# Moving the low parts of all split weights to VectorE, with a new port rule and other planned durations, in a windowed attention and MLP kernel

## The chip, the cores and the metric

The kernel runs on one core of a Trainium2 chip. The time is the device time of one execution in microseconds (us), the median of several runs. Engine names in the profile: PE is TensorE, PEld its weight loads, DVE is VectorE, ACT is ScalarE, POOL is GpSimd, SP is SyncE, which issues all DMAs. "L459" is line 459 of the kernel's file.

## The reference, cut to what matters

Inputs: q, k, v of (4, 8, 768, 64) in fp32, eight memory keys and values per head, and two weight matrices, w_in of (512, 2048) and w_out of (2048, 512).

```
for each chunk c of 32 queries:
    keys, values = 8 memory rows + rows (c*32 - 16) to (c*32 + 40), cut at the ends
    a = exp(scores - max);  a = a / (sum(a) + 1e-9)        scores = q k^T / 8
    attention[c] = a @ values
x = attention as (3072 tokens, 512)
h = x @ w_in;  g = s * relu(h)^2 + b;  out = g @ w_out      all fp32
```

## The kernel before, in words

**Data.** Attention is done in blocks of 96 queries against 128 keys (three chunks and a mask), two heads and four blocks at a time: that is one `attend(ch, c)`. Tokens are in eight chunks of 384 (`ch`), each of which needs four `attend` calls (`c`). The MLP runs over 16 blocks `f` of 128 hidden units; a step `(ch, f)` has a first product (`hidden`, L472, 12 matmuls) and a second (`result`, L494, 9 matmuls).

**Split in two parts.** The MLP's products are made of fp32r operands, each fp32 value being kept as a high part, rounded by a copy on ACT, and a low part, the value less its high part. There are three matmuls for each product: low by high, high by low, high by high. So there are low parts of x (L394, DVE), of g (L483, DVE) and of the weights (L459, DVE or POOL).

**Weights.** They come as 64-bit words (the host's arrays are viewed as int64 and passed as they are). `weight(i, half, f, due)` makes one tile of 128 x 512 from them: a DMA (L447), a scaled copy of the high word on ACT (L449, `wscale`), three integer operations on DVE (L450 `wlow`, L452 `wjoin`, L454 `wsign`), the high part on ACT (L458, `whigh`) and the low part (L459). There are 32 such tiles: half 0 is w_in, half 1 is w_out. In the kernel before, the low part is taken by DVE for the eight tiles of half 0 with f under 8, and by POOL (under the name `wrest`) for the other 24. The source words live in a ring of four buffers, the joined fp32 values in a ring of three (`wv`), which a tile holds from L449 to L459. Sixteen of the finished tiles lie in slots that earlier held source data.

**Attention.** One `attend` has score matmuls (L371), mask, maximum and shift in one custom DVE operation (L402), an exponential on ACT (L406), then for the normalisation a small POOL operation (L409), a reciprocal on DVE (L411) and a product on POOL (L412, `norm`). The probabilities are turned by PE and copied (L421, L424, L426) for the first two chunks, and by DVE block transposes (L432) for the others. Then come the value matmuls (L388) and the two parts of x (L393, L394). g is made by four ACT operations (L479 to L482) and one on DVE (L483).

**Order.** The instructions of each engine are in the order in which a planner written in the kernel (`Plan.lay`) lays them out, while the kernel is built. Each operation has an engine, a duration (`HOLD`), a priority (small is urgent) and dependences; a result is usable on another engine `LATE` ns after its operation's end. At each moment the planner goes through PE, ACT, DVE, POOL, SP, and gives an engine that is free its most urgent ready operation whose buffers can be had. Operations marked `lock` (L409, L412, the weights' operations on DVE, and L459) are those that need the SBUF port that DVE and POOL share; the planner never lays a locked operation of one of the two while a locked one of the other runs. On the chip nothing enforces that order between the two engines but data dependences: each engine runs its own list in order.

**Priorities.** A step's products and its g have its number u in the list of steps as priority (`result` 1.9 later). Steps are: chunk 0 with f 0 to 7 (u 0 to 7), chunk 1 with f 0 to 15 (u 8 to 23), chunk 0 with f 8 to 15, then the chunks 2 to 7. A weight tile has f + half - 1.5, so every weight is more urgent than the g of a step from u = 15 on, and those of f are more urgent than the g of step 8 + f. The normalisations of chunk 1 have -1.25 to 5.25, those of chunk 2 from 16.75 on. Until 40 us of the plan, empty moments of PE are filled with matmuls of no use (L296).

Of the kernel before, what the change touches and what calls it, by code (L numbers as in the profile page):

```python
# [52 lines left out]
         + [(ch, f) for ch in range(2, NCHUNK) for f in range(NF)])  # L53


HOLD = dict(hidden=527, result=705, scores=225, turn=110, value=165, warm=215, sums=470, total=950,
            relu=388, square=388, affine=570, high=388, xhigh=388, wscale=571, whigh=536, copy=270, exp=386, keep=388, store=480, bias=500,
            low=475, affine_v=475, rec=100, max=212, flip=316, xlow=470, wlow=336, wjoin=600, wsign=605, out=600,
            small=120, norm=1000, wrest=1250, issue=440)
LATE = dict(PE=200, ACT=150, DVE=130, POOL=100, SP=0)  # L60
RATE, LAND = 400.0, 2000.0
FLIGHT = 8
BEGIN = dict(PE=2500.0, ACT=2500.0, DVE=2500.0, POOL=2500.0, SP=800.0)
# [47 lines left out]
class Plan:  # L111
# [5 lines left out]
    def op(self, eng, kind, prio, fn, reads=(), writes=(), lock=False, size=0):  # L117
        o = Op()
        o.eng, o.hold, o.fn, o.prio, o.lock, o.n, o.size = eng, HOLD[kind], fn, prio, lock, len(self.ops), size
        o.deps, o.outs, o.vals = set(), [], []  # L120
# [16 lines left out]
    def lay(self, filler=None):  # L137

        for o in self.ops:
            o.left, o.ready, o.start = len(o.deps), 0.0, None  # L140
            for d in o.deps:
                d.outs.append(o)
        engines = ["PE", "ACT", "DVE", "POOL", "SP"]
        free = dict(BEGIN)
        lock = {"DVE": 0.0, "POOL": 0.0}
        waiting = {e: [] for e in engines}
        ready = {e: [] for e in engines}
        events = sorted(BEGIN.values())
        wire, flying = 0.0, []
        laid = []  # L150
        back = []
        for o in self.ops:
            if not o.left:
                heapq.heappush(waiting[o.eng], (0.0, o.n, o))
        todo = len(self.ops)
        while todo:
            t = heapq.heappop(events)
            while events and events[0] <= t:
                heapq.heappop(events)
            while back and back[0][0] <= t:  # L160
                v = heapq.heappop(back)[-1]
                v.ring.back(v)
            for e in engines:
                while waiting[e] and waiting[e][0][0] <= t:
                    o = heapq.heappop(waiting[e])[2]
                    heapq.heappush(ready[e], (o.prio, o.n, o))
                if free[e] > t:
                    continue
                if e == "SP":
                    flying = [x for x in flying if x > t]  # L170
                    if len(flying) >= FLIGHT:
                        heapq.heappush(events, min(flying))
                        continue
                put, got = [], None
                while ready[e]:
                    x = heapq.heappop(ready[e])
                    o = x[2]
                    new = [v for v in o.vals if v.slot is None and v.ring.tiles is not None]
                    held = o.lock and e in lock and lock["POOL" if e == "DVE" else "DVE"] > t
                    given = []  # L180
                    for v in new if not held else ():
                        if not v.ring.can(v):
                            break
                        v.ring.give(v)
                        given.append(v)
                    if not held and len(given) == len(new):
                        got = o
                        break
                    for v in reversed(given):
                        v.ring.undo(v)  # L190
                    if held:
                        heapq.heappush(events, lock["POOL" if e == "DVE" else "DVE"])
                    put.append(x)
                for x in put:
                    heapq.heappush(ready[e], x)
                if got is None:
                    if e == "PE" and filler and filler[0](t):
                        laid.append((t, -1, filler[1]))
                        free[e] = t + HOLD["warm"]
                        heapq.heappush(events, free[e])  # L200
                    continue
                o = got
                o.start = t
                free[e] = t + o.hold
                o.end = free[e] + LATE[e]
                if o.size:
                    wire = max(wire, t) + o.size / RATE
                    o.end = wire + LAND
                    flying.append(o.end)
                if o.lock and e in lock:  # L210
                    lock[e] = free[e]
                laid.append((t, o.n, o.fn))
                todo -= 1
                heapq.heappush(events, free[e])
                for d in o.outs:
                    d.left -= 1
                    d.ready = max(d.ready, free[e] if d.eng == e and not o.size else o.end)
                    if not d.left:
                        heapq.heappush(waiting[d.eng], (d.ready, d.n, d))
                        heapq.heappush(events, d.ready)  # L220
                for v in o.vals:
                    v.left -= 1
                    v.done = max(getattr(v, "done", 0.0), o.end)
                    if not v.left and v.ring.tiles is not None:
                        heapq.heappush(back, (v.done, o.n, o.vals.index(v), v))
                        heapq.heappush(events, v.done)
            if not events and todo:
                stuck = [(o.eng, o.prio, [v.kind for v in o.vals if v.slot is None]) for e in engines for _, _, o in ready[e]]
                raise AssertionError(f"the plan is stuck at {t}: {todo} left, {stuck[:12]}")
        self.end = max(o.end for o in self.ops)  # L230
        laid.sort(key=lambda x: (x[0], x[1]))
        return laid
# [3 lines left out]
def body(ctx: ExitStack, tc: tile.TileContext, qkv, w1, w2, s_in, b_in, out):  # L236
    nc = tc.nc
    plan = Plan()
    op = plan.op
# [14 lines left out]
    def weight_tile(half, f):  # L254
        if (half, f) not in wts:
            i = LATE_W.index((half, f)) if (half, f) in LATE_W else -1
            wts[half, f] = const.tile([P, 2, DM], F32R, name=f"w{half}_{f}", tag=f"slot{i}" if i >= 0 else f"w{half}_{f}")
        return wts[half, f]
# [180 lines left out]
    def weight(i, half, f, due):  # L439
        src = (w1, w2)[half][f]  # L440
        raw = Early(i, 0, 2 * DM) if i < NEARLY - 6 else Val(words)
        v, w = Val(wvs), c_w[half, f]
        both = lambda: raw.tile.bitcast(I32).rearrange("p (n two) -> p n two", two=2)
        lo, hi = (lambda: both()[:, :, 0]), (lambda: both()[:, :, 1])
        bits = lambda: v.tile.bitcast(I32)
        dst = lambda a: weight_tile(half, f)[:, a, :]
        op("SP", "issue", due - 4, lambda: nc.sync.dma_start(both(), src), (), (raw["lo"], raw["hi"]), size=P * DM * 8)  # L447

        op("ACT", "wscale", due, lambda: nc.scalar.activation(v.tile, hi().bitcast(F32), AF.Copy, scale=2.0 ** -112), (raw["hi"],), (v[0],))  # L449
        op("DVE", "wlow", due, lambda: nc.vector.tensor_scalar(lo(), lo(), 29, None, ALU.logical_shift_right),  # L450
           (), (raw["lo"],), lock=True)
        op("DVE", "wjoin", due, lambda: nc.vector.scalar_tensor_tensor(bits(), bits(), 3, lo(), ALU.logical_shift_left, ALU.bitwise_or),  # L452
           (raw["lo"],), (v[0],), lock=True)
        op("DVE", "wsign", due, lambda: nc.vector.scalar_tensor_tensor(bits(), hi(), -2147483648, bits(), ALU.bitwise_and, ALU.bitwise_or),  # L454
           (raw["hi"],), (v[0],), lock=True)
        rest = half or f >= N0
        old = list(c_early[LATE_W.index((half, f))].parts.values()) if (half, f) in LATE_W else []
        op("ACT", "whigh", due, lambda: nc.scalar.activation(dst(0), v.tile, AF.Copy), (v[0],), [w["H"], *old])  # L458
        op(("DVE", "POOL")[rest], ("wjoin", "wrest")[rest], due, lambda: (nc.vector, nc.gpsimd)[rest].tensor_tensor(  # L459
            dst(1), v.tile, dst(0).bitcast(F32), ALU.subtract), (v[0], w["H"]), (w["L"],), lock=True)  # L460


# [57 lines left out]
    for i, (due, half, f) in enumerate(ORDER):  # L520
        weight(i, half, f, due - 1.5)
# [49 lines left out]
```

## Time and profile before

| | |
|---|---|
| median of 3 runs | 658.1 us (657.54 to 658.69) |
| the profiled execution | 656.1 us, span 654.3 us |
| mean granted clock of TensorE | 0.992 of full speed |
| busy in the span: PE, DVE, ACT, POOL | 97%, 55%, 64%, 19% |

The profiled execution is one run; its span goes from the first to the last instruction, and 1.8 us of its time lie around the span. Busy shares over the span hide that the stages have different limits.

### The profile page before, as it was taken

To read this page: it belongs to the slowest core of one execution; us is meant where nothing else is said; L and a number is where in the kernel's file an instruction comes from. 1 tells how busy PE (TensorE), PEld (TensorE's weight loads), DVE (VectorE), ACT (ScalarE), POOL (GpSimd) and SP (SyncE) were. 2 spreads that over 40 slices of the span, in tenths; PEclk is the share of its full clock that TensorE was granted. 3 is DMA by queue.
4 is the path that set the end of the run, shared out by engine and by line. 5 is a ranking of instruction groups with operands and counts; after the bars stand their busy time and mean duration, and the time that the engine had idled before them with its cause. 6 is when DMAs were issued, how large, how long until landed. Compare 5 with 4: busy or idle time off the path is not lost.

```text
span 654.3 us, 10859 instructions
## 1 busy us (share of the span) xinstructions
PE 636.6 (97%) x3833; PEld 548.4 (84%) x3833; DVE 357.4 (55%) x1258; ACT 421.4 (64%) x1137; POOL 121.5 (19%) x168
## 2 busy tenths in 40 slices
PE   9999877999999999999999999999999999999996
PEld 5677766888888888888888888888888888889995
DVE  5899979872255545565455545555454655441112
ACT  6999898755466655566665656666655666655442
POOL 5544544340011011111101011110101111100000
PEclk9999989899999999999999999999999999999999
DMA  8933654200202110120112111021110210010001
GB/s 295 404 146 111 207 174 157 82 1 0 82 30 93 44 46 20 42 89 33 46 46 81 38 35 46 29 94 45 45 43 19 94 29 16 2 49 1 1 1 49
DMA packets 17623, 46.84 MB, mean 72 GB/s; under 512 B 2208, under 2 KB 2208, under 8 KB 17568
## 3 DMA queue, kind: packets, MB, share of 16 engines
q1 hardware_dynamic: 17568, 46.15, 20.6%
q8 instruction: 30, 0.49, 0.3%
q14 instruction: 25, 0.20, 0.1%
HBM read 39.85 MB, written 6.29 MB: 71 GB/s over the span
## 4 chain that ended last, share of the span: by engine, by line
PE 84%; DVE 7%; ACT 5%; DMA 2%; issue 1%; POOL 0%; SPq 0%; DVEq 0%; ACTq 0%
PE ps L494 37%; PE ps L472 37%; PE ps L371 5%; PE ps L388 4%; DVE wv L454 2%; DVE wv L452 2%; PE ps L296 1%; ACT t L406 1%; DVE words L450 1%; DMA early<-qkv 1%; ACT w L458 1%; PE ps L421 1%; ACT ps L481 1%; DMA words<-w 1%; ACT wv L449 1%
## 5 line engine op out<-in xcount | busy, mean ns | idle before, releaser
L472 PE MATMUL ps<-xH,w 128*128 128x384 f32 x1024 | 262.7, 338 | 1.5 <-DVE w L459 1.5
L494 PE MATMUL ps<-w,gH 128*128 128x512 f32 x768 | 242.1, 397 | 0.0
L472 PEld LDWEIGHTS ps<-xH,w 128*128 128x128 f32 x1024 | 187.1, 189 | 7.5 <-DVE w L459 2.0
L472 PE MATMUL ps<-xL,w 128*128 128x384 f32 x512 | 177.2, 346 | 0.0
L494 PEld LDWEIGHTS ps<-w,gH 128*128 128x128 f32 x768 | 145.6, 190 | 28.1
L494 PE MATMUL ps<-w,gL 128*128 128x512 f32 x384 | 156.2, 407 | 7.6 <-DVE gL L483 7.6
L479 ACT ACTIVATE ps<-ps 128x384 f32<-128x384 f32 x128 | 60.8, 475 | 150.8 <-PE ps L472 150.7
L483 DVE TENSOR_TENSOR gL<-ps,gH 128x384 fp32r<-128x384 f32 x128 | 71.3, 557 | 132.8 <-ACT gH L482 130.6
L432 DVE STREAM_TRANSPOSE aT<-t 32x128 f32<-32x128 f32 x384 | 116.2, 302 | 50.2 <-POOL t L412 45.5
L406 ACT ACTIVATE t<-t,nmax 96x128 f32<-96x128 f32 x256 | 99.1, 391 | 9.4 <-DVE nmax L402 9.4
L472 PEld LDWEIGHTS ps<-xL,w 128*128 128x128 f32 x512 | 96.8, 189 | 9.0 <-ACT w L458 0.3
L494 PEld LDWEIGHTS ps<-w,gL 128*128 128x128 f32 x384 | 72.6, 189 | 24.5 <-DVE gL L483 9.6
L402 DVE CUSTOM_DVE_ANT_0 t<-ps,mask 96x128 f32<-96x128 f32 x256 | 58.9, 280 | 56.6 <-PE ps L371 55.6
L481 ACT ACTIVATE ps<-ps,b_sb,s_sb 128x384 f32<-128x384 f32 x128 | 82.5, 644 | 4.1
L412 POOL TENSOR_TENSOR t<-t,rden 96x512 f32<-96x512 f32 x64 | 69.4, 1086 | 65.5 <-DVE rden L411 65.5
L409 POOL TENSOR_SCALAR rden<-den 96x4 f32<-96x4 f32 x64 | 15.7, 245 | 331.8 <-ACT t L406 329.1
L482 ACT ACTIVATE gH<-ps 128x384 fp32r<-128x384 f32 x128 | 62.8, 491 | 3.6
L480 ACT ACTIVATE ps<-ps 128x384 f32<-128x384 f32 x128 | 60.9, 476 | 3.8
L406 ACT ACTIVATION_READ_ACCUMULATOR t<-t,nmax 96x1 f32 x256 | 48.7, 190 | 0.0
L459 POOL TENSOR_TENSOR w<-wv,w 128x512 fp32r<-128x512 f32 x24 | 33.1, 1385 | 53.3 <-ACT w L458 53.3
L393 ACT ACTIVATE xH<-ps 128x384 fp32r<-128x384 f32 x32 | 15.7, 490 | 41.3 <-PE ps L388 40.8
L371 PE MATMUL ps<-raw 64*96 64x128 f32 x448 | 32.5, 280 | 0.0
(47 smaller groups left out, 321.8 us busy)
## 6 DMA issues: line engine op xcount, KB each, us to landing
raw<-qkv SPq DMA_DIRECT2D x28, 448.0 KB, 3.4
words<-w SPq DMA_DIRECT2D x22, 512.0 KB, 3.5
v<-qkv SPq DMA_DIRECT2D x28, 256.0 KB, 2.7
out<-partial SPq DMA_DIRECT2D x21, 256.0 KB, 2.6
early<-w SPq DMA_DIRECT2D x10, 512.0 KB, 9.4
early<-qkv SPq DMA_DIRECT2D x4, 448.0 KB, 6.5
early<-qkv SPq DMA_DIRECT2D x4, 256.0 KB, 6.8
out<-wv SPq DMA_DIRECT2D x3, 256.0 KB, 2.0
```

What stands on the lines that cost most here:

```text
L371: nc.tensor.matmul(scv(n)[:, j, :], raw.tile[rows, j * QB:(j + 1) * QB], raw.tile[rows, TOK + j * P:TOK + (j + 1) * P], start=True, stop=True)
L402: op("DVE", "max", a + 0.1, lambda j=j: nc.vector.tensor_tensor_reduce(t.tile[:, j, :], scv()[:, j, :], mask[:, half, j], -SCALE, 3.0e38, ...
L406: op("ACT", "exp", a + 0.2, lambda j=j: nc.scalar.activation(t.tile[:, j, :], t.tile[:, j, :], AF.Exp, bias=nmax()[:, j:j + 1], scale=-1.0 ...
L412: op("POOL", "norm", a + 0.25, lambda: nc.gpsimd.tensor_tensor(t.tile, t.tile, rden().unsqueeze(2).to_broadcast([QB, GB, P]), ALU.mult), [ ...
L432: nc.vector.transpose(aT.tile[gg, :, cs], t.tile[cs, :, gg])
L472: nc.tensor.matmul(h.tile[:, :TOK], weight_tile(0, f)[:, wi, c * P:(c + 1) * P], x.tile[xi], start=(c == 0 and n == 0), stop=(c == NC_T - ...
L479: op("ACT", "relu", u, lambda: nc.scalar.activation(hp(), hp(), AF.Relu), (), (h[0],))
L480: op("ACT", "square", u, lambda: nc.scalar.activation(hp(), hp(), AF.Square), (), (h[0],))
L481: op("ACT", "affine", u, lambda: nc.scalar.activation(hp(), hp(), AF.Identity, scale=s_sb, bias=b_sb), (c_s[0], c_b[0]), (h[0],))
L482: op("ACT", "high", u, lambda: nc.scalar.activation(g.tile[0], hp(), AF.Copy), (h[0],), (g["H"],))
L483: op("DVE", "low", u, lambda: nc.vector.tensor_tensor(g.tile[1], hp(), g.tile[0].bitcast(F32), ALU.subtract), (h[0], g["H"]), (g["L"],))
L494: nc.tensor.matmul(acc.tile, g.tile[gi][:, t * P:(t + 1) * P], weight_tile(1, f)[:, wi, :], start=(first and n == 0), stop=(last and n == 2))
```

## The change

All 32 low parts of weights (L459) are on DVE, under the planner's name `wjoin`. The planner gets a rule: a locked operation of DVE or POOL is put back if the other of the two engines is free and has a ready locked operation with a smaller priority. `HOLD` and `LATE` are changed in some 15 places: `turn`, `value`, `small`, `rec`, `hidden` and others a few to 120 ns, and `LATE` up by 30 to 50 ns. `rest` is left without use.

```
-            low=475, affine_v=475, rec=100, max=212, flip=316, xlow=470, wlow=336, wjoin=600, wsign=605, out=600,
-            small=120, norm=1000, wrest=1250, issue=440)
-LATE = dict(PE=200, ACT=150, DVE=130, POOL=100, SP=0)
+            low=475, affine_v=475, rec=120, max=212, flip=316, xlow=470, wlow=345, wjoin=610, wsign=612, out=600,
+            small=240, norm=1010, wrest=1290, issue=440)
+LATE = dict(PE=230, ACT=180, DVE=180, POOL=150, SP=0)
...
-                    held = o.lock and e in lock and lock["POOL" if e == "DVE" else "DVE"] > t
+                    other = "POOL" if e == "DVE" else "DVE"
+                    held = o.lock and e in lock and lock[other] > t
+
+                    if o.lock and e in lock and free[other] <= t and any(y[2].lock and y[:2] < x[:2] for y in ready[other]):
+                        put.append(x)
+                        continue
...
-        op(("DVE", "POOL")[rest], ("wjoin", "wrest")[rest], due, lambda: (nc.vector, nc.gpsimd)[rest].tensor_tensor(
+        op("DVE", "wjoin", due, lambda: nc.vector.tensor_tensor(
             dst(1), v.tile, dst(0).bitcast(F32), ALU.subtract), (v[0], w["H"]), (w["L"],), lock=True)
```

In the first line of `HOLD`, `hidden` goes from 527 to 535, `result` from 705 to 712, `scores` from 225 to 222, `turn` from 110 to 84 and `value` from 165 to 185.

## Rows read from the trace of the kernel before

**Rows 1.** Windows by stage: PE, PEld, DVE, ACT, POOL busy, clock, DMA share, GB/s.

```profile
40.00:76.00 36.00, 34.20 (x228) 28.02 (x228) 34.40 (x103) 34.48 (x97) 17.68 (x17) 1.00 0.38 127
76.00:136.00 60.00, 50.12 (x264) 43.08 (x263) 50.84 (x108) 47.12 (x121) 26.98 (x23) 0.91 0.39 131
136.00:649.00 513.00, 512.24 (x3021) 451.23 (x3020) 240.26 (x898) 307.42 (x804) 57.51 (x91) 1.00 0.12 39
```

**Rows 2.** Waits of PE from 76 to 136 us: total, times, longest.

```profile
PE ps L494 <- DVE gL L483: 6.8, 4, 2.7
PE ps L388 <- DVE gL L483: 1.7, 1, 1.7
```

**Rows 3.** Timeline of PE, the matmuls that follow its longest gaps.

```profile
81.32 0.38 PE L388 MATMUL ps<-aT,v 128*64 128x96 f32 x2 [1.66 <-DVE gL L483]
...
90.68 0.50 PE L494 MATMUL ps<-w,gL 128*128 128x512 f32 x1 [2.14 <-DVE gL L483]
...
112.88 0.80 PE L494 MATMUL ps<-w,gL 128*128 128x512 f32 x1 [2.74 <-DVE gL L483]
...
135.53 0.50 PE L494 MATMUL ps<-w,gL 128*128 128x512 f32 x1 [1.29 <-DVE gL L483]
```

**Rows 4.** Windows with the clock below full, columns as in rows 1.

```profile
100.00:120.00 20.00, 16.60 (x69) 14.31 (x69) 18.84 (x52) 15.08 (x43) 7.92 (x7) 0.83 0.34 119
...
114.00:116.00 2.00, 2.00 (x6) 1.55 (x5) 1.93 (x12) 2.00 (x5) 0.51 (x2) 0.50 0.32 115
```

**Rows 5.** Groups of instructions by line: busy us, mean ns, idle before and its releaser.

```profile
L459 POOL TENSOR_TENSOR w<-wv,w 128x512 fp32r<-128x512 f32 x24 | 33.1, 1385 | 53.3 <-ACT w L458 53.3
L459 DVE TENSOR_TENSOR w<-wv,w 128x512 fp32r<-128x512 f32 x8 | 5.5, 684 | 0.0
```

**Rows 6.** The weights' DVE operations by line: shortest, median and longest ns.

```profile
L450 DVE TENSOR_SCALAR words<-words x22: 415/423/1530, 46.0 to 132.1; 128x512 int32<-128x512 int32 x22
L452 DVE SCALAR_TENSOR_TENSOR wv<-wv,words x22: 676/686/1595, 56.8 to 132.6; 128x512 int32<-128x512 int32 x22
L454 DVE SCALAR_TENSOR_TENSOR wv<-words,wv x22: 681/693/1800, 57.5 to 133.4; 128x512 int32<-128x512 int32 x22
```

**Rows 7.** Timeline of DVE: a moved operation's pace, and operations beside POOL.

```profile
46.05 1.86 DVE L450 TENSOR_SCALAR words<-words 128x512 int32<-128x512 int32 x2
...
71.15 0.68 DVE L459 TENSOR_TENSOR w<-wv,w 128x512 fp32r<-128x512 f32 x1
71.75 0.28 DVE L402 CUSTOM_DVE_ANT_0 t<-ps,mask 96x128 f32<-96x128 f32 x1
...
73.86 1.41 DVE L454 SCALAR_TENSOR_TENSOR wv<-words,wv 128x512 int32<-128x512 int32 x1
...
76.52 1.52 DVE L450 TENSOR_SCALAR words<-words 128x512 int32<-128x512 int32 x1
78.14 1.59 DVE L452 SCALAR_TENSOR_TENSOR wv<-wv,words 128x512 int32<-128x512 int32 x1
...
133.35 1.66 DVE L454 SCALAR_TENSOR_TENSOR wv<-words,wv 128x512 int32<-128x512 int32 x1
134.93 0.55 DVE L483 TENSOR_TENSOR gL<-ps,gH 128x384 fp32r<-128x384 f32 x1
```

**Rows 8.** Timeline of POOL beside the operations of rows 7.

```profile
73.24 1.49 POOL L412 TENSOR_TENSOR t<-t,rden 96x512 f32<-96x512 f32 x1
76.02 3.17 POOL L459 TENSOR_TENSOR w<-wv,w 128x512 fp32r<-128x512 f32 x2 [1.29 <-ACT w L458]
```

**Rows 9.** Waits of DVE and of ACT from 76 to 136 us.

```profile
DVE gL L483 <- ACT gH L482: 4.9, 4, 2.1
...
ACT w L458 <- DVE wv L454: 8.5, 7, 2.2
```

**Rows 10.** Windows of L459, then of L412, alone: busy time and count, DVE then POOL.

```profile
76.00:136.00 60.00, 0.00 (x0) 22.86 (x17) 0.91 0.39 131
...
40.00:136.00 96.00, 11.41 (x9) 0.95 0.38 130
```

More of the change, by code (lines that the diff above doesn't have):

```diff
@@ L53 @@
          + [(ch, f) for ch in range(2, NCHUNK) for f in range(NF)])
-HOLD = dict(hidden=527, result=705, scores=225, turn=110, value=165, warm=215, sums=470, total=950,
+HOLD = dict(hidden=535, result=712, scores=222, turn=84, value=185, warm=215, sums=470, total=950,
             relu=388, square=388, affine=570, high=388, xhigh=388, wscale=571, whigh=536, copy=270, exp=386, keep=388, store=480, bias=500,
-            low=475, affine_v=475, rec=100, max=212, flip=316, xlow=470, wlow=336, wjoin=600, wsign=605, out=600,
-            small=120, norm=1000, wrest=1250, issue=440)
-LATE = dict(PE=200, ACT=150, DVE=130, POOL=100, SP=0)
+            low=475, affine_v=475, rec=120, max=212, flip=316, xlow=470, wlow=345, wjoin=610, wsign=612, out=600,
+            small=240, norm=1010, wrest=1290, issue=440)
+LATE = dict(PE=230, ACT=180, DVE=180, POOL=150, SP=0)
 RATE, LAND = 400.0, 2000.0
@@ L191, in lay @@
                     if held:
-                        heapq.heappush(events, lock["POOL" if e == "DVE" else "DVE"])
+                        heapq.heappush(events, lock[other])
                     put.append(x)
```

## The prediction

> **What bounds the kernel now.** I read the stages first, since 97% busy over the whole span says nothing about one stage. From 136 to 649 us PE is busy for 512.24 of 513 us at full clock [rows 1]: nothing that DVE or POOL gain there can move the end, and only the last weight operation reaches into it. What can be won or lost lies before. From 40 to 76 us PE, DVE and ACT are all full (34.20, 34.40 and 34.48 of 36 us). From 76 to 136 us PE has only 50.12 of 60 us, at a mean clock of 0.91, while DVE still has 50.84 and ACT 47.12 [rows 1]. So this stage loses 9.9 us of PE to waits and 60 x 0.09 = 5.4 us to the clock, about 15 us together; that is the whole prize, apart from the first 40 us.
>
> Next I read who is waited for. From 76 to 136 us 8.5 us are for the low part of g (L483 on DVE), five times [rows 2]. The timeline puts them in a few gaps: 1.66, 2.14, 2.74 and 1.29 us [rows 3], and one of 0.7 us that is left of the sum, at 101 us. The clock falls behind the two longest: 0.83 from 100 to 120 us [rows 4], which is 20 x 0.17 = 3.4 us, and the other 2 us behind the gap that ends at 90.68 us. Before the fall PE had stood idle, and the first matmul after the 2.74 us gap takes 0.80 us where its like after other gaps take 0.50 [rows 3]. PE at half clock, 0.50 from 114 to 116 us [rows 4], 1.2 in place of 2.4 GHz, is the second price of a gap.
>
> Then why L483 is late. Two low parts of weights on POOL (76.02 us, 3.17 us for both [rows 8]) run beside two operations of DVE that take 1.52 and 1.59 us [rows 7], where their medians are 0.42 and 0.69 [rows 6]: DVE stood still for 1.1 + 0.9 = 2.0 us, with L483 queued behind. So with a like pair at 108 us, before the longest gap, and in a smaller way at 133.35 us, where a 0.69 us operation takes 1.66 us and L483 starts right behind it [rows 6, 7]. From 76 to 136 us there are nine such rows, with 8.7 us over the medians in all; one more is at 46 us, where two L450 take 1.86 us [rows 7], some 1.1 us over two that run alone. The second chain is ACT's: it waits 8.5 us for L454 [rows 9], which these stretches delay, and L483 then waits 4.9 us for ACT's high part.
>
> **The change, part by part.**
>
> *Low parts to DVE.* POOL loses 24 operations of 1385 ns, 33.1 us [rows 5]. DVE gets 24 of 684 ns; the next operation starts 0.60 us after such a one (71.15 to 71.75 [rows 7]), so they cost its queue 24 x 0.60 = 14.4 us. It gets back the 9.8 us of stretches. Net: 4.6 us more on DVE. This has to be split by stage.
>
> Seven of the 24 lie before 76 us and 17 behind [rows 10]. The seven: 7 x 0.60 = 4.2 us more, 1.1 us back, so 3.1 us more in a stage where DVE has 36 - 34.40 = 1.6 us free [rows 1]. What doesn't fit is 1.5 us at least, 3.1 us if no free moment can be used; PE is nearly full here as well, with work that is due soon, so I charge it: +2 us, between 1.5 and 3.1.
>
> The 17: 17 x 0.60 = 10.2 us more, 8.7 us back, 1.5 us more, against 9.2 us in which DVE has nothing to run [rows 1]. The load fits. What counts is when. A stretch of 2.0 us for two low parts becomes 1.2 us of DVE work that the planner knows of and can lay behind L483, or ahead of it. The gaps whose cause is a stretch are 1.66, 0.7, 2.74 and 1.29 us, 6.4 us, with 3.4 us of clock after the longest: 9.8 us. If the new operations all stand in front of L483, 40% of it (0.8 of 2.0) comes back, 3.9 us; if none does, all of it. Weights are more urgent to the planner than most of these g, which speaks for the lower end; but a shorter gap may also spare the clock, which is a step and not a slope. I take two thirds: -6.5 us, between -3.9 and -9.8.
>
> *A new wait.* A low part on DVE waits for ACT's high part (L458) at the head of DVE's queue, where POOL could stand idle for 53.3 us at no cost; behind it stand L402 and L483, and PE waits for these. The eight that are on DVE now found their input ready: 0.0 idle [rows 5]. I take nothing for it, as those eight; the upper bound is a wait like L458's own, 8.5 / 7 = 1.2 us [rows 9], for a few of them.
>
> *Normalisations.* They stay on POOL. They stretch DVE too: 1.41 for 0.69 us at 73.86 us, beside L412 taking 1.49 us [rows 7, 8]. With a fuller DVE a few more meet; there are nine between 40 and 136 us [rows 10], so from 0 to 9 x 0.7 = 6 us of DVE, of which the trace shows about 3 already. I take 0 more, and the rest goes to the range. The port is thus one thing that either engine holds at a time: the 1.52 us operation begins 0.5 us after POOL's pair and ends after POOL's first. The Trainium skill (SBUF — State Buffer, Who interferes with whom) has it that the second to issue blocks fully until the first is done, also for a DVE operation with two SBUF inputs; the stretch of 1.1 us agrees. By that rule the moved operations can themselves be blocked, at the price just bounded.
>
> *The port rule and the other durations.* Before, the planner looks at DVE first, so a run of weight operations could keep an urgent normalisation back in the plan, though not on the chip. Now it is laid earlier, and PE's turn and value matmuls with it. The changes of 10 to 120 ns reorder single operations. No row prices a reordering. The bound from both sides is the worst single gap with its clock, 2.74 + 3.4 = 6.1 us; I take 0, since PE's long stage has 0.8 us idle in 513 and each g has two steps of slack.
>
> *Queues.* SP's weight DMAs wait for L454 to free a word buffer; with fewer stretches they start earlier, into a DMA share of 0.39 [rows 1]. The joined values' buffers are held for 0.7 in place of 1.4 us at the end. Both are cover, not gain. No DMA is added.
>
> Sum: +2 - 6.5 = -4.5 us. The profiled execution has 656.1 us (span 654.3), so 651.6 us on its scale; it is 2.0 us below the median of the runs, 658.1 us, and the change is put on that: **653.6 us**.
>
> **Rivals.**
>
> *Slower: DVE becomes the bound.* The weights end at 136 us because DVE's queue ends then. Its load rises by 4.6 us, and from 40 to 76 us there is no room. If the phase is as long as DVE's work, with the same idle moments, PE loses 4.6 us plus a new 1.2 us wait: 658.1 + 5.8 = 663.9 us. For it: 34.40 of 36 us [rows 1], and weights going ahead of L483. Against: 9.2 us free later, and that most of what is added replaces standing still. It decides where DVE has under 4 us free between 76 us and the last weight. The Trainium skill (Perfetto Trace Analysis, Optimizing Scalar/DVE Operations) says that with DVE saturated it may make sense to move work off to GpSimd, which speaks against this change; it adds that between these two, which share a port, it might not help. The 9.8 us of stretches bear out the second half.
>
> *No change: ACT sets the pace.* ACT is 34.48 of 36 us busy and 47.12 of 60 [rows 1], nothing of it is removed, and the 2.14 us gap comes while L483 itself waits for ACT [rows 3, 9]. If L483 waits for ACT wherever DVE is faster, the 3.9 us of the lower end less 2 to 3.1 us remain: -0.8 to -1.9, about 657 us. The same comes out if the port rule hardly fires.
>
> *Much faster: the clock never falls.* If all gaps from stretches go, and both falls of the clock with them (5.4 us), the gain is 6.4 + 5.4 = 11.8 us, with the first stage's +2 repaid by earlier normalisations: 646 us.
>
> **How the numbers follow.** A measurement of this kernel tells about 0.2%, 1.3 us, from no change. Forecast 0.40 (650 to 656.5), much faster 0.15, ACT 0.17 (of which 0.03 below the bound and 0.01 above), DVE the bound 0.28. Faster 0.40 + 0.15 + 0.03 = 0.58; slower 0.28 + 0.01 = 0.29; same 0.13. The range of 8 in 10 reaches from 645 (the clock case) to 664 (DVE the bound). If the sign is right, 645 to 656.5.
>
> **What would show it.** Right: no long rows at L450, L452 and L454 but beside L412; DVE busy up by some 4 us before the weights end, and that end before 136 us; the waits for L483 from 8.5 to some 4 us; the clock above 0.91 from 76 to 136 us; 136 us to the end unchanged. Wrong: PE waiting for L459 or L483 between 40 and 76 us, DVE idle in front of L459 with ACT's L458 as releaser, gaps in the long stage, or a new gap of over 2 us with the clock at half.

## The result and the profile after

The changed kernel takes 649.24 us (median of 4 runs, 649.05 to 649.31) against 657.82 us for the kernel before on the same chip (656.27 to 658.69): a ratio of 0.9872, 95% interval 0.9853 to 0.9891. It is 8.6 us faster, where 4.5 us had been forecast; 649.2 lies in the range. The profiled execution has 649.26 us with a span of 647.4 us, and a mean clock of 0.999 (before: 0.992).

All lines behind the planner's have moved by five: L459 of before is L464, L483 is L488, L494 is L499, L472 is L477, and the integer operations L450, L452, L454 are L455, L457, L459.

The stages of the changed kernel, with the columns of [rows 1]:

```profile
0.00:40.00 40.00, 37.90 (x325) 25.38 (x326) 28.68 (x144) 32.01 (x118) 20.68 (x37) 1.00 0.90 334
40.00:76.00 36.00, 33.59 (x236) 27.39 (x235) 34.28 (x103) 35.20 (x102) 11.35 (x12) 1.00 0.35 112
76.00:136.00 60.00, 54.21 (x276) 46.79 (x275) 56.19 (x131) 48.95 (x109) 5.07 (x7) 1.00 0.39 132
136.00:640.00 504.00, 504.00 (x2996) 443.80 (x2994) 238.13 (x903) 306.27 (x812) 55.20 (x88) 1.00 0.13 41
```

The reader is to see three things. The long stage is as it was: PE without a gap. From 76 to 136 us PE is busy for 54.21 in place of 50.12 us and its clock no longer falls (1.00 for 0.91): 4.1 + 5.4 = 9.5 us won. The two overlap a little, since PE also stood idle at half clock: taken in windows of 1 us, the clock cost 4.7 us of PE's busy time, and 8.8 us is the closer sum. DVE went from 50.84 to 56.19 us there, so it is now the fullest engine of that stage. From 40 to 76 us PE has 0.6 us less.

What PE waits for, first from 40 to 76 us, then from 76 to 136 us:

```profile
PE ps L477 <- DVE w L464: 1.9, 2, 1.2
...
PE ps L499 <- DVE gL L488: 5.8, 7, 1.3
```

Five waits for the low part of g, 8.5 us in all [rows 2], have become seven with 5.8 us; the longest gap is 1.26 us where it was 2.74 us [rows 3]:

```profile
101.33 0.50 PE L499 MATMUL ps<-w,gL 128*128 128x512 f32 x1 [0.86 <-DVE gL L488]
...
107.00 0.50 PE L499 MATMUL ps<-w,gL 128*128 128x512 f32 x1 [1.26 <-DVE gL L488]
```

The operations that replaced those of [rows 5], and the integer operations to be held against [rows 6], by line:

```profile
L464 DVE TENSOR_TENSOR w<-wv,w x32: 678/684/693, 28.9 to 123.0; 128x512 fp32r<-128x512 f32 x32
...
L455 DVE TENSOR_SCALAR words<-words x22: 393/421/847, 59.1 to 118.1; 128x512 int32<-128x512 int32 x22
...
L457 DVE SCALAR_TENSOR_TENSOR wv<-wv,words x22: 677/692/703, 59.6 to 118.6; 128x512 int32<-128x512 int32 x22
...
L459 DVE SCALAR_TENSOR_TENSOR wv<-words,wv x22: 658/692/694, 60.8 to 119.3; 128x512 int32<-128x512 int32 x22
```

No moved operation is longer than 693 ns, and the longest of these integer operations fell from 1530, 1595 and 1800 ns to 847, 703 and 694. The long ones that are left behind 40 us, this 847 ns one and two of 1110 and 1320 ns at 44 and 58 us on tiles outside these rows, each run beside a normalisation on POOL. The last low part starts at 123.0 us, where it was 135.8 us on POOL: the weights are done some 13 us sooner, with 4.6 us more work on DVE's account. The engine and the order both changed, and so the first question for the experiments is: is it the engine, or the new order?

### The profile page after: what moved, and what is told of

Read it like the earlier page. It is cut to its first block, busy times and chain, and to the rows that moved or that the text cites. A ratio compares the mean times of both kernels' runs of the same rounds, so it can differ in the third digit from the quotient of the medians.

```text
span 647.4 us, 10853 instructions
## 1 busy us (share of the span) xinstructions
PE 632.2 (98%) x3836; PEld 545.0 (84%) x3836; DVE 359.9 (56%) x1282; ACT 422.7 (65%) x1137; POOL 92.3 (14%) x144
## 4 chain that ended last, share of the span: by engine, by line
PE 85%; ACT 6%; DVE 6%; DMA 1%; issue 1%; SPq 0%; DVEq 0%
PE ps L499 38%; PE ps L477 37%; PE ps L376 5%; PE ps L393 4%; DVE wv L459 2%; DVE wv L457 2%; PE ps L301 1%; ACT wv L454 1%; DVE w L464 1%; ACT w L463 1%; DMA early<-qkv 1%; ACT ps L486 1%; ACT t L411 1%; PE ps L426 1%; ACT ps L485 1%
## 5 line engine op out<-in xcount | busy, mean ns | idle before, releaser
L477 PE MATMUL ps<-xH,w 128*128 128x384 f32 x1024 | 261.8, 337 | 1.9 <-DVE w L464 1.9
L499 PE MATMUL ps<-w,gH 128*128 128x512 f32 x768 | 240.1, 394 | 0.3 <-DVE w L464 0.3
L477 PEld LDWEIGHTS ps<-xH,w 128*128 128x128 f32 x1024 | 186.1, 188 | 8.0 <-DVE w L464 2.8
L477 PE MATMUL ps<-xL,w 128*128 128x384 f32 x512 | 176.4, 344 | 0.0
L499 PEld LDWEIGHTS ps<-w,gH 128*128 128x128 f32 x768 | 144.2, 188 | 28.6 <-DVE w L464 0.7
L499 PE MATMUL ps<-w,gL 128*128 128x512 f32 x384 | 154.8, 403 | 6.6 <-DVE gL L488 6.6
L484 ACT ACTIVATE ps<-ps 128x384 f32<-128x384 f32 x128 | 60.8, 475 | 135.2 <-PE ps L477 135.2
L488 DVE TENSOR_TENSOR gL<-ps,gH 128x384 fp32r<-128x384 f32 x128 | 71.2, 556 | 112.5 <-ACT gH L487 110.3
L411 ACT ACTIVATE t<-t,nmax 96x128 f32<-96x128 f32 x256 | 99.2, 391 | 10.7 <-DVE nmax L407 10.6
L477 PEld LDWEIGHTS ps<-xL,w 128*128 128x128 f32 x512 | 96.0, 188 | 8.9 <-ACT w L463 0.2
L499 PEld LDWEIGHTS ps<-w,gL 128*128 128x128 f32 x384 | 72.0, 188 | 23.8 <-DVE gL L488 9.2
L414 POOL TENSOR_SCALAR rden<-den 96x4 f32<-96x4 f32 x64 | 19.6, 306 | 364.8 <-ACT t L411 362.5
L399 DVE TENSOR_TENSOR xL<-ps,xH 128x384 fp32r<-128x384 f32 x32 | 17.7, 555 | 35.5 <-ACT xH L398 35.5
```

The lines of the kernel that those rows point to most:

```text
L411: op("ACT", "exp", a + 0.2, lambda j=j: nc.scalar.activation(t.tile[:, j, :], t.tile[:, j, :], AF.Exp, bias=nmax()[:, j:j + 1], scale=-1.0 ...
L477: nc.tensor.matmul(h.tile[:, :TOK], weight_tile(0, f)[:, wi, c * P:(c + 1) * P], x.tile[xi], start=(c == 0 and n == 0), stop=(c == NC_T - ...
L484: op("ACT", "relu", u, lambda: nc.scalar.activation(hp(), hp(), AF.Relu), (), (h[0],))
L488: op("DVE", "low", u, lambda: nc.vector.tensor_tensor(g.tile[1], hp(), g.tile[0].bitcast(F32), ALU.subtract), (h[0], g["H"]), (g["L"],))
L499: nc.tensor.matmul(acc.tile, g.tile[gi][:, t * P:(t + 1) * P], weight_tile(1, f)[:, wi, :], start=(first and n == 0), stop=(last and n == 2))
```

## The experiments

Twelve kernels were run, each timed against the kernel before on the same chip. "Loss" is what PE lost from 40 to 136 us in the profiled execution: its idle time plus (1 - clock) x length of the stages. It leaves out the first 40 us, and counts idle time at half clock one and a half times.

| kernel | median us | ratio, 95% interval | loss us |
|---|---|---|---|
| before | 657.2 (19 runs) | 1 | 11.7 + 5.4 |
| changed | 649.24 | 0.9872, 0.9853 to 0.9891 | 8.2 + 0 |
| e1 engine, order of before | 651.67 | 0.9924, 0.9907 to 0.9940 | 9.5 + 1.8 |
| e2 order of the changed one, GpSimd | 652.74 | 0.9942, 0.9922 to 0.9962 | 10.7 + 0 |
| e3 engine, planned anew | 648.49 | 0.9879, 0.9861 to 0.9898 | 7.4 + 1.7 |
| e4 rule and durations | 648.21 | 0.9873, 0.9856 to 0.9889 | 6.7 + 0 |
| e5 rule | 650.35 | 0.9893, 0.9861 to 0.9925 | 8.3 + 0 |
| e6 durations | 655.35 | 0.9976, 0.9964 to 0.9987 | 11.5 + 3.6 |
| e7 before, nudged | 657.21 | 1.0004, 0.9991 to 1.0016 | 12.7 + 3.6 |
| e8 changed, nudged | 649.08 | 0.9874, 0.9859 to 0.9890 | 8.4 + 0 |
| e9 changed, weights less urgent | 643.82 | 0.9796, 0.9777 to 0.9815 | 3.8 + 0 |
| e10 = e4, weights less urgent | 645.46 | 0.9820, 0.9804 to 0.9836 | 4.6 + 0 |
| e11 before, weights less urgent | 651.39 | 0.9902, 0.9886 to 0.9919 | 9.5 + 1.8 |
| e12 = e3, weights less urgent | 648.34 | 0.9855, 0.9840 to 0.9870 | 6.1 + 3.2 |

### Engine and order, held apart

The planner makes it possible to change the engine that issues an operation and keep every list in its order: the plan is made for one engine, and another issues.

e1, the plan of before, issued by DVE:

```
-        op(("DVE", "POOL")[rest], ("wjoin", "wrest")[rest], due, lambda: (nc.vector, nc.gpsimd)[rest].tensor_tensor(
+        op(("DVE", "POOL")[rest], ("wjoin", "wrest")[rest], due, lambda: nc.vector.tensor_tensor(
```

> The order of the kernel before is kept on every engine; only the 24 low parts are issued by VectorE, at the place that the plan gave to GpSimd. Theory H (the gain is that VectorE no longer stands still beside GpSimd): the long rows of L450, L452 and L454 beside L459 go (8.7 us from 76 to 136 us), the clock falls behind long gaps go, time about 650 to 653 us. Rival R (the gain is the new order, in which the weights are laid without the attention of chunk 2 between them): 656 us or more, as DVE's load rises by 4.6 us and new waits for the high part of ACT stand at the head of its queue.

e2, the plan of the changed kernel, issued by POOL:

```
-        op("DVE", "wjoin", due, lambda: nc.vector.tensor_tensor(
+        op("DVE", "wjoin", due, lambda: (nc.vector, nc.gpsimd)[rest].tensor_tensor(
```

> The order of the changed kernel is kept on every engine; only the 24 low parts are issued by GpSimd again, as before. Theory H: each runs 1.3 us beside a VectorE that never pauses, so most of them stretch VectorE by some 0.7 to 1.0 us where it saved 0.6 us of work; weights end some 5 us later than in the changed kernel, time 654 to 660 us. Rival R: 649 to 651 us, as the order is what counts, and GpSimd is otherwise idle in that stretch.

e1 gains 5.1 us (651.67 against 656.78 in that session), as theory H expected. e2, 652.74 us, lies between its two cases: it gains 4.0 us over the kernel before, and is 3.5 us slower than the changed kernel (4.6 us by the ratios, as the two were timed in different sessions). So with the order fixed, the move off POOL is worth 5.1 us in the old order and 3.5 to 4.6 us in the new one. The new order, with the engine fixed, is worth 4.0 us on POOL and 2.4 to 3.4 us on DVE, which theory H had at nothing. In e1, the stage by windows, and from PE's timeline the longest gap that is left:

```profile
76.00:136.00 60.00, 51.74 (x283) 44.02 (x282) 54.91 (x134) 49.10 (x124) 9.44 (x12) 0.97 0.40 131
```

```profile
88.18 0.63 PE L494 MATMUL ps<-w,gL 128*128 128x512 f32 x1 [2.15 <-DVE gL L483]
```

DVE's 54.91 us hold 17 low parts more, 10.2 us by the forecast's 0.60 us each, and the total rose by only 4.1 us over [rows 1]. The same 46 integer operations take 28.4 us in this stage (L450, L452 and L454 together) where they took 36.8, so 8.4 us of stretches are gone. More than half of it is L454's (windows of this line alone, before and then e1):

```profile
76.00:136.00 60.00, 15.73 (x16) 0.91 0.39 131
...
76.00:136.00 60.00, 11.20 (x16) 0.97 0.40 131
```

The 2.74 us gap of before, ahead of the same matmul, is one of 1.49 us, while the 2.14 us one, which waits for ACT's chain, is still there with 2.15 us (L483 waits 1.1 us for ACT there).

In e2 the low parts on POOL as a group, and one pair beside DVE (timelines of POOL and of DVE):

```profile
L464 POOL TENSOR_TENSOR w<-wv,w 128x512 fp32r<-128x512 f32 x24 | 37.0, 1554 | 36.0 <-ACT w L463 35.8
```

```profile
90.51 3.18 POOL L464 TENSOR_TENSOR w<-wv,w 128x512 fp32r<-128x512 f32 x2 [2.36 <-ACT w L463]
...
91.48 1.05 DVE L455 TENSOR_SCALAR words<-words 128x512 int32<-128x512 int32 x1
92.63 1.61 DVE L457 SCALAR_TENSOR_TENSOR wv<-wv,words 128x512 int32<-128x512 int32 x1
```

Both engines pay: the POOL operations take 1554 ns in the mean where they took 1385 [rows 5], and the DVE operations beside them 1.05 and 1.61 us for medians of 0.42 and 0.69 [rows 6]. The gaps come at each step (seven from 0.43 to 1.36 us), but none is long, and the clock stays at 1.00.

### Parts of the change, planned anew

e3 changes only the engine, in the plan too; the diff is the last two lines of the change's. e4 takes the rest of the change and leaves those two lines out.

> The kernel before with all low parts given to VectorE in the plan too, but without the port rule and with the durations of before. Theory H: most of the gain, 649 to 653 us. Rival (the port rule or the durations make the gain): over 655 us.

> The port rule and the new durations alone; the 24 low parts stay on GpSimd, in the plan too. Theory H: little, 655 to 660 us, with the long rows of L450, L452 and L454 still there. Rival (rule or durations make the gain): under 653 us.

e3 has all of the gain and comes out a little under theory H's 649 to 653 us. But e4 has all of it too, without the move, where 655 to 660 us were expected: theory H falls as the only cause. Beside the rule and the durations, the move adds nothing that these runs can tell (ratios of 0.9873 for e4 and 0.9872 for the changed kernel). e4's stage, and in its groups by line the third integer operation:

```profile
76.00:136.00 60.00, 56.44 (x284) 48.38 (x282) 55.06 (x101) 49.47 (x113) 28.51 (x25) 1.00 0.41 135
```

```profile
L459 DVE SCALAR_TENSOR_TENSOR wv<-words,wv 128x512 int32<-128x512 int32 x22 | 23.9, 1087 | 0.6
```

It takes 1087 ns in the mean, where the kernel before has 974 and the changed kernel 690, and PE is still busy for 56.44 us. So the stretches are all there, as theory H expected, and in this order they cost little. That a stretch costs what stands behind it, and not its length, is the reading that e9 and e10 will test.

e5 and e6 split e4: the port rule alone, and the durations alone. e7 and e8 ask how much of all this is chance in the planner's order: one planned duration is made 2 ns longer, `hidden` 529 for 527 in the kernel before and 537 for 535 in the changed one.

> The port rule alone, with the low parts on GpSimd and the durations of before. e4 gave 648.2 with rule and durations; theory D (the durations make it): 655 to 658 us here. Theory P (the port rule makes it, since urgent normalisations are no longer kept back): 648 to 651 us.

> The new durations alone, with the low parts on GpSimd and no port rule. Theory D: 648 to 651 us. Theory P: 655 to 658 us. If both e5 and e6 give 650 us or less, the plan of before is merely an unlucky one and any new order is better (theory L).

> The kernel before with one planned duration 2 ns longer (hidden 529 for 527), which tells the planner nothing. Theories D and P: the time of before within 2 us, 655 to 659 us. Theory L: another order, 648 to 653 us.

> The changed kernel with one planned duration 2 ns longer (hidden 537 for 535). If its gain is of the change and not of one lucky order: 648 to 651 us. Theory L allows anything from 646 to 656 us.

The nudged kernels take the time of their originals (657.21 and 649.08 us). But the traces show that a nudge hardly moves anything: by line and tile, e8 has the very order of the changed kernel on PE, DVE, ACT and POOL, and in e7 one operation of DVE, one of ACT and two short runs of PE's matmuls stand elsewhere. So e7 and e8 show that the times repeat, and not whether the order of the change is a lucky one among many; that stays open. Theory L's other half, that any new order is better, falls by e6, whose order is new and gains 1.9 us.

The rule alone gives 6.9 us (650.35 against 657.24) and the durations alone 1.9 us (655.35), the times of theory P. The reason that it named, urgent normalisations kept back without the rule, no run separates from the rest; PE's waits agree with it. The kernel before has gaps of 1.66 and 1.39 us ahead of the value matmuls L388 at 81 and 83 us, behind the low part of g and behind the turned probabilities. Both are gone in e5, while e1, in the old order, keeps one of 1.17 us.

e5 shows more. Its four runs, with the granted clock of each:

```
648.72 us, 1.000    652.21 us, 0.994    651.98 us, 0.994    648.36 us, 1.000
```

It is one kernel with two outcomes, 3.6 us apart (652.1 less 648.5), and the clock tells them apart: 0.006 of 650 us is 3.9 us. The slower runs were not profiled. Its profiled execution, one of the 1.000 runs, has this longest gap:

```profile
92.26 0.50 PE L499 MATMUL ps<-w,gL 128*128 128x512 f32 x1 [2.21 <-DVE gL L488]
```

Seven profiles have a fall of the clock between 40 and 136 us. Their longest gaps of PE are 2.74 us (before), 2.15 (e1), 2.80 (e3), 2.76 (e6), 2.77 (e7), 2.17 (e11) and 2.83 (e12). In the seven without a fall they are 1.26 us (changed), 1.36 (e2), 1.31 (e4), 2.21 (e5), 1.25 (e8), 1.11 (e9) and 0.90 (e10). The fall costs 1.7 or 3.4 us of clock each time, by (1 - clock) x length. But it doesn't stand behind each long gap. In e7 there is none behind the longest:

```profile
113.66 0.50 PE L494 MATMUL ps<-w,gL 128*128 128x512 f32 x1 [2.77 <-DVE gL L483]
```

```profile
113.00:119.00 6.00, 5.34 (x26) 4.79 (x27) 5.84 (x23) 5.91 (x16) 2.33 (x2) 1.00 0.29 90
```

Nor does each fall lengthen a kernel: e1's four runs have clocks of 0.996, 0.998, 0.997 and 1.000 and agree within 0.25 us. So a long gap costs its length, and in some executions more at half clock, as the 3.6 us between e5's outcomes.

How the rule works is shown in part only. Of DVE's block transposes, which belong to the attention of chunk 2, 16 lie between 76 and 120 us in the kernel before and in e1, 8 in e4 and e5, none in e3 and the changed kernel (windows of the transposes' line alone, before and then e5):

```profile
76.00:120.00 44.00, 4.82 (x16) 0.88 0.46 154
```

```profile
76.00:120.00 44.00, 2.42 (x8) 1.00 0.54 178
```

So both parts of the change do the same thing to the plan: weights go first, and the attention of chunk 2, which is not due, goes behind them. The count doesn't set the time: e9 and e10 below, the fastest kernels of all, have 16 and 28 of these transposes there. What moves the transposes back is argued from the code: without the rule, a low part on POOL waits in the plan behind DVE's integer operations of later tiles, since DVE is asked first, and then locks DVE out, which fills the time with unlocked work of low urgency; with the rule, or with no low part on POOL, that doesn't arise. It was not tried by itself. It would explain why the parts don't add: 8.3 us (e3) and 8.6 us (e4) alone, 8.6 us together.

### What is left: where the low part of g stands

In the changed kernel, ACT's last operation for this g, and then DVE's timeline around the 1.26 us gap:

```profile
103.09 0.49 ACT L487 ACTIVATE gH<-ps 128x384 fp32r<-128x384 f32 x1
...
104.46 0.69 DVE L457 SCALAR_TENSOR_TENSOR wv<-wv,words 128x512 int32<-128x512 int32 x1 [0.46 <-ACT wv L454]
105.19 0.69 DVE L459 SCALAR_TENSOR_TENSOR wv<-words,wv 128x512 int32<-128x512 int32 x1
105.80 0.68 DVE L464 TENSOR_TENSOR w<-wv,w 128x512 fp32r<-128x512 f32 x1
106.40 0.55 DVE L488 TENSOR_TENSOR gL<-ps,gH 128x384 fp32r<-128x384 f32 x1
106.86 0.68 DVE L464 TENSOR_TENSOR w<-wv,w 128x512 fp32r<-128x512 f32 x1
```

L488, for which PE stands idle, has its input at 103.6 us and starts 2.8 us later, behind a weight's operations. The same holds ahead of all seven gaps: L457, L459 and L464 run in front of L488, which has had its input for 0.5 to 2.8 us. e9 makes the weights of f from 8 on five steps less urgent; they are needed from step 16 on.

```
 FLIGHT = 8
+LATER = 5.0
...
-        weight(i, half, f, due - 1.5)
+        weight(i, half, f, due - 1.5 + (f >= N0) * LATER)
```

> The changed kernel, with the weights of f from 8 on five steps less urgent (they are not needed before step 16), so that the low part of g is laid ahead of them. If the 5.8 us that PE still waits for L488 from 76 to 136 us are its place behind weight operations: most of them go, 643 to 646 us, and the weights end later, up to 135 us. If VectorE's load itself is the bound there (56.2 of 60 us): 648 to 651 us, the gaps only move.

e10 is the same edit on e4, e11 on the kernel before, e12 on e3.

> The same with the 24 low parts on GpSimd, in the plan too. If only the place in VectorE's queue counts: 643 to 647 us, like e9. If stretches beside GpSimd still cost: 2 us or more above e9.

> The kernel before, with nothing of the change, but the weights of f from 8 on five steps less urgent. If the place of the low part of g behind weight operations is what all the gaps come from: 644 to 648 us, so most of the gain is had without the change. If the low parts on GpSimd without the port rule still come in bursts that stretch VectorE: 651 us or more.

> All low parts on VectorE and the weights of f from 8 on five steps less urgent, without the port rule and with the durations of before. If rule and durations add nothing once both are done: 642 to 645 us, like e9. If they still matter: 646 us or more.

e9 takes 643.82 us, its first case and the fastest of all: 5.4 us better than the changed kernel (5.0 by the ratios). Its stage, and PE's longest item of waits over the whole span (L500 and L489 are L499 and L488 of the changed kernel):

```profile
76.00:136.00 60.00, 58.51 (x299) 51.34 (x299) 55.89 (x132) 50.82 (x113) 5.11 (x7) 1.00 0.39 130
```

```profile
PE ps L500 <- DVE gL L489: 2.2, 5, 0.8
```

DVE is as full as in the changed kernel (55.89 and 56.19 us), and PE has 58.51 us. From 76 to 136 us PE now waits 1.5 us for the low part of g, where it waited 5.8, and each starts at most 0.7 us after its input. The last low part of a weight starts at 127.1 us. So it was not DVE's load that held PE, but what stood in front of L488. With this cured, the move off POOL is worth 1.6 us (e9 against e10, 645.46 us, in one session); e10 is within its first case, under 2 us above e9. The integer operations are still stretched in e10, L458 for instance to 16.40 us for 17 where e9's 16 take 11.06.

e11 gives 651.39 us, its second case: the priority alone is worth 6.3 us in the kernel before, so 644 to 648 us, most of the gain, was too much to expect of it; with the change it makes 13.9 us (e9). Without the rule, and with the low parts on POOL, two integer operations of 1.67 and 1.63 us beside POOL still stand ahead of the low part of g (L484 in e11) at 110 us. Another gap, of 1.60 us at 91.7 us, is not from POOL: there DVE is idle for 0.8 us in front of L484, which waits for ACT's high part. Three of e11's gaps:

```profile
81.72 0.38 PE L389 MATMUL ps<-aT,v 128*64 128x96 f32 x2 [1.32 <-DVE gL L484]
...
83.44 1.54 PE L389 MATMUL ps<-aT,v 128*64 128x96 f32 x14 [1.34 <-ACT aT L425]
...
110.84 0.50 PE L495 MATMUL ps<-w,gL 128*128 128x512 f32 x1 [2.17 <-DVE gL L484]
```

The clock falls behind the first two, which lie close together (0.57 from 83 to 87 us), and not behind the longest one (1.00 from 110 to 116 us).

e12, 648.34 us, takes its second case, 646 us or more; it is no better than e3. Its time goes to one gap of PE, and to the clock in the window behind it (L473 and ACT's L459 are L472 and L458 of the kernel before):

```profile
72.75 0.51 PE L473 MATMUL ps<-xL,w 128*128 128x384 f32 x1 [2.83 <-ACT w L459]
```

```profile
72.00:80.00 8.00, 6.50 (x33) 5.49 (x33) 6.22 (x13) 5.62 (x13) 0.00 (x0) 0.57 0.59 197
```

PE waits 2.83 us for ACT's high part of a weight of f under 8, which the new priority doesn't touch, and runs at 0.57 of the clock from 72 to 80 us, 3.4 us. ACT in turn waits 1.5 us for an integer operation of 1.41 us on DVE, beside a normalisation on POOL. e3 has the same gap (2.80 us), e9 and the changed kernel do not. Rule and durations, which are all that e9 has beyond e12, are worth 4.5 us here (3.9 by the ratios).

## Why the prediction was right, and where it was not

**The bound: right.** All of the change lies before 136 us; PE's long stage is untouched, and the windows that were named as the prize (15 us) gave it.

**The load: right.** DVE's added work was put at 14.4 us less 9.8 us of stretches. In the order of before (e1), the integer operations from 76 to 136 us take 8.4 us less, of 8.7 us that were forecast. DVE's busy time there rose by 4.1 us where 1.5 us was forecast, as five more transposes and other operations now fall into the stage; it is still within the 9.2 us that were free.

**The first stage: sign right, size not.** +2 us were charged from 40 to 76 us, and PE lost 0.6 us more (36 - 33.59 against 36 - 34.20). DVE stayed as full, 34.28 us: ten low parts lie in the stage where five did, and 46 of the attention's operations L402 where there were 52.

**The second stage: the term that was mis-sized.** -6.5 us, between -3.9 and -9.8, was forecast, and 4.1 us of idle time and 5.4 us of clock came back, 9.5 us (8.8 without the overlap). Of the clock I took two thirds of one fall, where both went whole. The text had said that the clock is a step and not a slope, and then took a fraction of it; e5's two outcomes, 3.6 us apart, show the step. The idle time fell less than the stretches' 6.4 us would give, since L488 still stands behind weights, as the text had feared; e9 confirms that part. One of the gaps in these 6.4 us, that of 0.7 us, was also read wrongly: L483 starts 0.2 us after its input there, so it waits for ACT and not behind a stretch.

**The rule and the durations: wrong.** They were put at 0, "since PE's long stage has 0.8 us idle in 513 and each g has two steps of slack". That looked at the wrong stage. The rule alone gives 6.9 us and the durations 1.9 us. The bound of 6.1 us that was kept for the reordering was nearly the right size, and the text didn't use it: an order that decides which operation stands in front of L488 is worth nearly as much as the stretches themselves. So the forecast had the right stage, the right mechanism for one half of the change, and missed that the other half is a second way to the same gain. That the time came out in the range in spite of this is in part luck: the two halves, 8.3 and 8.6 us alone, don't add. Had they added, the time would have been some 641 us, below the range.

**The new wait: right at nothing.** DVE was idle in front of L464 twice in all of the span, for 1.5 us together.

**The rivals.** DVE as the bound didn't come, though its own sign did: under 4 us free between 76 us and the last weight was named as the point from which it decides, and DVE had 1.8 us free there (45.90 of 47.70 us busy up to 123.7 us). The sign was a wrong one. In e9 DVE has 1.4 us free up to its last weight at 127.8 us, and PE is busy for 50.74 of these 51.80 us. The rival counted DVE's load, and what counted was its order. The rule quoted there from the Trainium skill (Perfetto Trace Analysis, Optimizing Scalar/DVE Operations), that moving work from a full VectorE to GpSimd may make sense but might not help because of the shared port, comes out on its second half: 3.5 to 5.1 us are lost by the offload with the order fixed. Planned anew, with the rule, it costs between nothing (e4) and 1.6 us (e10). ACT as the pace didn't come either; its wait for DVE's third integer operation fell from 8.5 us [rows 9] to 4.6 us as DVE got quicker. The case "the clock never falls" came nearest: it named 646 us, and its clock half came in full, while 4.1 of its 6.4 us of idle time did.

On its own scale the profiled execution moved from 656.1 to 649.3 us, 6.8 us: 8.8 us in the second stage, less 0.6 us in the first, less 1.1 us of PE idle in the first 40 us, where a wait for a DMA took 1.3 us; 0.3 us stay open. The medians differ by 8.6 us because the runs of before vary by 2.4 us, with the profiled one, 656.1 us, below them, and those of the changed kernel by 0.3 us.

## What to carry to other kernels

Price a stalled operation by what stands behind it in its engine's queue: moving the low parts off POOL was worth 5.1, 3.5 or 1.6 us depending on the order, and nothing against e4, which had all the stretches. Where a planner lays the queues, its rules for shared resources and its priorities are part of the machine: look which operation stands in front of the one that the bound engine waits for, and change that before moving work between engines. Count a gap of PE with the clock that can fall behind it, as a step that comes in some executions and not in others.

## What the runs showed that was not expected

The clock makes one kernel have two times: e5 gave 648.4 and 648.7 us with the clock at 1.000, and 652.0 and 652.2 us with 0.994, on the same chip in the same session. In 19 runs the kernel before had 655.3 to 658.4 us at clocks from 0.990 to 0.995, so none of them escaped the fall, while the changed kernel, e2, e4 and e9, with no gap over 1.4 us, repeat to within 0.7 us. A fall need not cost time, though: e1, with a gap of 2.15 us, repeats to within 0.25 us at clocks from 0.996 to 1.000.

On the shared port both sides pay: a low part on GpSimd took 1554 ns in the mean in e2 and 1338 ns in e4, with VectorE about as busy from 76 to 136 us (56.48 and 55.06 us). What makes the difference between the two was not tried.
